# Another order of a chunk's cycle, and other moments for its loads, in an attention and expert kernel

## The chip, the cores and the metric

The kernel runs on one core of a Trainium2 chip. The metric is the device time of one execution in microseconds, launch to end, as the median of several runs. "Us" below are microseconds.

## What is computed

The reference is windowed causal attention with a linear bias over 8 batches of 8 heads, 576 positions and 64 dimensions, followed by a layer of 8 experts, of which each token goes to the one that its gate ranks first:

```python
scores = scale * np.matmul(q, k.transpose(0, 1, 3, 2))
bias = slopes[:, None, None] * (-np.abs(rel).astype(np.float32))[None, :, :]
mask = (rel >= 0) & (rel < 128)
attn = softmax(np.where(mask, scores + bias[None], -1e9))
x = np.matmul(attn, v)                     # as rows: (4608 tokens, 512)
expert_idx, gate_w = argmax and softmax value of x @ w_gate
out[mask_e] = gate_w * (np.maximum(x[mask_e] @ w1[e], 0) @ w2[e])   # for each expert e
```

## The kernel before

Attention goes by 36 chunks of 128 query rows, all 8 heads together. A pair of batches makes nine chunks: four blocks of the first batch, one "tail" chunk that holds the last 64 rows of both batches, four blocks of the second. A query row looks back 127 positions, so a chunk needs its own key block and the one before; the first block of a batch (chunks 0, 5, 9, 14, 18, 23, 27, 32) has no block before it, so its scores and its values are half as large.

The order of every engine's instructions is written out by hand. The program counts steps, four for a chunk, and each piece of a chunk's work has a step relative to the chunk's first (a "lag") and a rank within the step. What stands in one step on several engines is recorded in the order of the ranks, and each engine then runs its own list in that order, waiting on semaphores alone. The work of several chunks thus interleaves; with c the chunk that begins in a cycle of four steps, one cycle holds:

- **S0** and **S1**, the scores of heads 0 to 3 and 4 to 7 of chunk c (`scores`, L163: bias from a bf16 matmul against an identity, then query times key), each into a PSUM bank pair of its own, `s0_ps` and `s1_ps`, which each serve every chunk.
- **F0** and **F1** (`weigh`, L191): VectorE folds the two key blocks into one with a masked copy (L196; none in a first block) and takes the maximum (L199). **E0** and **E1**: ScalarE's four exponentials each (L205), the sum with them. E1 goes in two halves, one in chunks from 3 on ahead of the x copy, one behind.
- **T0** of chunk c-1 and **T1** of chunk c-2 (`transposes`, L217), into one of the two banks `b_ps` that take turns; **P0** and **P1** (`place`): ScalarE copies a transposed half to `pT` (L223), GpSimd masks it into its two key blocks (two selects, L231 and L233; none in a first block).
- **V**, the values of chunk c-2 (`av`, L249), 32 matmuls (16 in a first block) into a third `b_ps`, the first half of them from P0, the second from P1. **X**: ScalarE's copy of that bank to `xT` (L299).
- **R** of chunk c-4 (`rows`, L263), which brings x to rows and adds the gate's logits, and **Y** (L266), VectorE's multiply by the reciprocal of the sums (L256), with the logits' sum (L1252) and the store of x to HBM (L1258).

With two banks `b_ps` and the order T1, T0, V, each T0 takes the bank that the V of the cycle before wrote and X reads.

Beside that runs routing: every five or six chunks (`GROUPS`) a group's tokens are ranked in four pieces on VectorE (`route`, L484), one at the end of each of four cycles running, with a few matmuls on TensorE. GpSimd adds a small guard to the sums (L189) and scales queries (L77). From step 57 on the first expert's weights are split into two parts, half a tile a cycle: a cast on ScalarE (L1042), its remainder on GpSimd (L1047).

Loads and x stores stand on SyncE's queue in program order, so a load behind an x store is asked for when Y has run. Before, a batch's keys are asked for four chunks ahead in one load (`KA = 16` steps), query tiles four chunks ahead (`QA = 4`), value tiles at most one and three quarters of a cycle ahead of their use (`VA = 4` against a lag of 11).

From about 210 us on the experts run: first layer and second layer of each of them, 128 to 512 columns a matmul.

Of the kernel before, what the change touches and what calls it, by code (L numbers as in the profile page):

```python
# [22 lines left out]
NP = H // 2  # L23
# [17 lines left out]
def attention(ctx, tc, st, qT, kT, v, iw, load_c2, chunk_done, chunks, begun):  # L41
# [95 lines left out]

    k0 = load_k(0, (0, KCUT, 256, 384, S))
    next(k0)
# [12 lines left out]
    next(k0)  # L152
# [3 lines left out]
    list(k0)  # L156
# [34 lines left out]
    def weigh(g, pe, rsum, s_ps, m, tail, lo, hi, later=False, add=True):  # L191
# [20 lines left out]
        return exps if later else exps()  # L212
# [41 lines left out]
    def rows(ch, subs, xT, rsum):  # L254
        rinv = small.tile([128, H], F32, name="rinv")
        nc.vector.reciprocal(out=rinv, in_=rsum)  # L256
        st["r_ps"] = r_ps = ps_r.tile([128, 2, 512], F32, name="r_ps")
        heads = r_ps[:, :, 0:NP * HW].rearrange("q c (p x) -> q p c x", p=NP)
        half = lambda c: slice(64 * c, 64 * c + 64)
        for p in range(NP):  # L260
            for a in range(2):
                for c in range(2):
                    nc.tensor.matmul(out=heads[half(a), p, c, :], lhsT=xT[half(c), p, half(a)], rhs=iw_sb[half(c), p, :],  # L263
                                     start=True, stop=True)
        x_sb = xp.tile([128, NP, XW], F32, name="x_sb")
# [5 lines left out]
    ahead = {}  # L271
    done_q, done_v, scaled = {(0, 0), (0, 1), (0, 2)}, {(0, 0), (0, 1)}, {(0, 0)}
    for ch, subs in enumerate(chunks):
        for b, i in subs:
            k = (b, i // 4)
            for seen, f, at in ((done_q, load_q, 4 * (ch - QA)), (done_v, load_v, 4 * ch + VA - TA * (k[1] == 4)),
                                (scaled, lambda b, m: scale_q(nc.gpsimd, b, m), 4 * ch - 6)):
                for j in ((b, 3), k) if f == load_v and k[1] == 4 else (k,):
                    if j not in seen:
                        seen.add(j)  # L280
                        ahead.setdefault(max(0, at), []).append((f,) + j)
# [3 lines left out]
    lags = lambda ch: LAGS.get(ch, LAGS[None])  # L285
    plan = {}
    for ch in range(len(chunks)):
        for k, at in enumerate(lags(ch)):
            plan.setdefault(4 * ch + at, []).append((k, ch))
        for k, at in enumerate(SUMS.get(ch, ())):  # L290
            plan.setdefault(4 * ch + at, []).append((11 + k, ch))
        if ch in SPLIT:
            plan.setdefault(4 * ch + 3, []).append((10, ch))
        plan.setdefault(4 * ch + lags(ch)[1] + (ch in SPLIT), []).append((13, ch))
    live, pes, sums, pTs, xTs, xps, second, turned = {}, {}, {}, {}, {}, {}, {}, {}
# [5 lines left out]
    def do(k, ch):  # L301
        if k == 9:
            return copy_x(ch)
        if k == 13:
            return place(chunks[ch], 0, turned.pop(ch), pTs[ch])
        if k > 10:
            h = slice(4 * k - 44, 4 * k - 40)
            nc.vector.tensor_reduce(out=sums[ch][:, h], in_=pes[ch][:, h, :], axis=AX.X, op=ALU.add)
            return guard(sums[ch]) if k == 12 else None
        if k == 10:  # L310
            exps = second.pop(ch)
            exps((0,))
            copy_x(ch - 2)
            return exps((1,))
        subs = chunks[ch]
        if k in (0, 4):
            if k == 0:
                pes[ch] = pp.tile([128, H, 128], F32, name="pe")
                sums[ch] = small.tile([128, H], F32, name="rsum", bufs=8)
            live[ch] = scores(subs, k // 4)  # L320
        elif k in (2, 5):
            second[ch] = weigh(k // 3, pes[ch], sums[ch], *live.pop(ch), later=k == 5 and ch in SPLIT, add=ch not in SUMS)
        elif k == 1:
            pTs[ch] = ptp.tile([128, 2, H, 128], F32, name="pT")
            turned[ch] = transposes(0, pes[ch])
        elif k == 3:
            rows(ch, subs, xTs.pop(ch), sums.pop(ch))
        elif k == 6:
            place(subs, 1, transposes(1, pes[ch] if ch in SUMS else pes.pop(ch)), pTs[ch])
        elif k == 7:  # L330
            xps[ch] = bank() if ch else ps_r.tile([128, 2, 512], F32, name="r_ps")[:, 0].rearrange("q (p x) -> q p x", p=NP)
            av(subs, pTs[ch], xps[ch], range(NP // 2))
        else:
            av(subs, pTs.pop(ch), xps[ch], range(NP // 2, NP))
            if len(lags(ch)) < 10 and ch + 2 not in SPLIT:
                copy_x(ch)

    def rank(k, ch, s):
        if k == 9:
            return 0.5  # L340
        if k == 6 and s == 4 * ch + 8:
            return 1
        if k == 1 and ch in SPLIT:
            return 1.5
        if k == 13:
            return 3.5 if ch in SPLIT else 1
        return 4.5 if k == 6 and s == 4 * ch + 6 else k

    def step(s):
# [5 lines left out]
        for f, b, m in ahead.get(s, ()):  # L355
            f(b, m)
        for k, ch in sorted(plan.get(s, ()), key=lambda x: (rank(*x, s), x[1])):
            do(k, ch)
        if s < len(WU) - 1:
            warm_up(WU[s + 1])  # L360
        for k in list(st["stages"]):
            if k[1] <= s and (s in PACE[k[2]] if k[2] in PACE else s % 4 == 3):
                k[1] = s + 1
                if next(k[0], k) is k:
                    st["stages"].remove(k)
# [21 lines left out]
LAGS = {None: (0, 4, 0, 17, 2, 2, 8, 11, 11)}  # L387
LAGS.update({ch: (0, 4, 0, 17, 2, 2, 6, 11, 11) for ch in (1, 2)})
LAGS[0] = (0, 4, 0, 17, 2, 2, 6, 7, 11, 12)
LAGS.update({ch: (0, 4, 0, 17, 2, 2, 8, 9, 11) for ch in (4, 13, 22, 31)})  # L390
LAGS.update({33: (0, 4, 0, 15, 2, 2, 8, 11, 11), 34: (0, 4, 0, 13, 2, 2, 8, 10, 10), 35: (0, 4, 0, 10, 2, 2, 6, 8, 8)})
# [3 lines left out]
TA = 4  # L395
# [12 lines left out]
KCUT = 128  # L408
# [9 lines left out]
QA = 4  # L418
KA = 16
# [903 lines left out]
```

## Time and profile before

| what | value |
| --- | --- |
| median of the runs | 639.75 us (lowest 639.19) |
| the profiled execution, whole | 640.18 us |
| its span, first to last instruction | 638.5 us |
| TensorE busy | 616.4 us, 97% |
| VectorE busy | 390.1 us, 61% |
| ScalarE busy | 313.9 us, 49% |
| GpSimd busy | 301.7 us, 47% |

The shares are averages over attention and experts. In the attention part, from 105 to 135 us for instance, VectorE, ScalarE and GpSimd are busy 79, 87 and 75% of the time, while a busy TensorE means only that matmuls follow each other: their ends are modelled, so a hole is best read from the starts of the groups on both sides of it. TensorE's granted clock is full (1.00) throughout attention. "Issue" in a row means that the engine waited for nothing that the profile shows.

### The profile page before, as it was taken

Reading aid. Unit: us, or ns where it says so; the run is one execution under the profiler, and the core shown is the slowest. Engines: PE = TensorE matmul, PEld = TensorE weight load, DVE = VectorE, ACT = ScalarE, POOL = GpSimd, SP = SyncE. Lnnn points to the kernel's source line nnn. Section 1 sums busy time; section 2 is a strip of 40 time slices with the busy share of each in tenths; the row PEclk is TensorE's granted clock in tenths of the full one; section 3 lists DMA queues with packets and bytes.
Section 4 is the critical chain, followed back from the end, with each engine's and each line's share of the span. In section 5 each row is a group of like instructions: output and inputs, shape, how many; then the busy total and the mean of one; then the engine's idle time right before and its main releaser. Section 6 shows DMA issues by size and latency. Waiting matters only on the chain.

```text
span 638.5 us, 16747 instructions
## 1 busy us (share of the span) xinstructions
PE 616.4 (97%) x6544; PEld 527.1 (83%) x6544; DVE 390.1 (61%) x946; ACT 313.9 (49%) x939; POOL 301.7 (47%) x414
## 2 busy tenths in 40 slices
PE   8998999999898999999999999999999999999995
PEld 5776777777676988988989999899899998888884
DVE  7677888859888886545553664565465456356411
ACT  5877788888777324533342334334233333433311
POOL 5643557768554150076327616732760760580202
PEclk9999999999999999999999999999999999999999
DMA  8967898988644253473535325433543542544101
GB/s 310 303 164 213 212 266 234 216 260 229 169 99 118 68 166 87 163 257 103 190 104 181 105 78 181 122 92 128 160 106 101 173 126 78 182 120 138 65 1 61
DMA packets 58179, 97.85 MB, mean 153 GB/s; under 512 B 11685, under 2 KB 32421, under 8 KB 57202
## 3 DMA queue, kind: packets, MB, share of 16 engines
q1 hardware_dynamic: 49618, 76.74, 40.2%
q0 software_dynamic: 8336, 19.76, 11.0%
q8 instruction: 52, 0.85, 0.6%
q10 hardware_dynamic: 144, 0.26, 0.2%
q14 instruction: 29, 0.24, 0.1%
HBM read 77.76 MB, written 18.98 MB: 152 GB/s over the span
## 4 chain that ended last, share of the span: by engine, by line
PE 67%; DVE 2%; ACT 1%; issue 0%; POOLq 0%; POOL 0%; ACTq 0%
PE y_ps L936 32%; PE l_ps L735 30%; PE s_ps L735 1%; PE x_ps L692 1%; PE b_ps L249 1%; PE y_ps L895 1%; PE r_ps L263 1%; DVE x_sb L266 0%; ACT pe L205 0%; PE b_ps L217 0%; DVE nmax L199 0%; DVE s_ps L196 0%; PE x_ps L895 0%; ACT xT L299 0%; PE s_ps L692 0%
## 5 line engine op out<-in xcount | busy, mean ns | idle before, releaser
L738 ACT ACTIVATE hh<-l_ps 128x320 fp32r<-128x320 f32 (+4 forms) x104 | 46.5, 447 | 200.7 <-PE l_ps L735 200.7
L742 DVE SCALAR_TENSOR_TENSOR hl<-l_ps,hh 128x320 fp32r<-128x320 f32 (+4 forms) x104 | 52.2, 502 | 147.7 <-ACT hh L738 147.4
L715 POOL DMA_INDIRECT xg<-xd,od_idx x112 | 117.6, 1050 | 35.2 <-issue 33.8
L205 ACT ACTIVATE pe<-s_ps,nmax 128x128 f32<-128x128 f32 x288 | 102.4, 382 | 36.2 <-DVE nmax L199 30.9
L936 PE MATMUL y_ps<-wh,hh 128*128 128x512 f32 x280 | 110.0, 393 | 0.0
L936 PE MATMUL y_ps<-wl,hh 128*128 128x512 f32 x280 | 109.4, 391 | 0.0
L936 PE MATMUL y_ps<-wh,hl 128*128 128x512 f32 x280 | 109.2, 390 | 0.0
L924 POOL DMA_INDIRECT out<-y,od_pidx x33 | 34.4, 1043 | 147.8 <-ACT y L942 141.3
L1030 DVE TENSOR_TENSOR wl<-w_raw,wh 128x512 fp32r<-128x512 f32 x114 | 73.7, 688 | 30.0 <-ACT wh L1026 29.7
L735 PE MATMUL l_ps<-xh,wh 128*128 128x320 f32 (+8 forms) x416 | 81.0, 316 | 0.0
L735 PE MATMUL l_ps<-xl,wh 128*128 128x320 f32 (+8 forms) x416 | 80.4, 315 | 0.0
L735 PE MATMUL l_ps<-xh,wl 128*128 128x320 f32 (+8 forms) x416 | 80.3, 315 | 0.0
L735 PEld LDWEIGHTS l_ps<-xh,wh 128*128 128x128 f32 x416 | 67.8, 188 | 6.7 <-issue 1.2
L735 PEld LDWEIGHTS l_ps<-xl,wh 128*128 128x128 f32 x416 | 65.9, 188 | 1.9
L735 PEld LDWEIGHTS l_ps<-xh,wl 128*128 128x128 f32 x416 | 65.8, 188 | 2.0
L249 PE MATMUL b_ps<-pT,v_sb 128*64 128x128 f32 (+2 forms) x1136 | 65.6, 265 | 0.8 <-issue 0.6
L249 PEld LDWEIGHTS b_ps<-pT,v_sb 128*64 128x64 f32 (+1 forms) x1136 | 56.4, 137 | 10.4 <-issue 5.8
L936 PEld LDWEIGHTS y_ps<-wh,hl 128*128 128x128 f32 x280 | 52.6, 188 | 11.5
L1026 ACT CAST wh<-w_raw 128x1024 fp32r<-128x1024 f32 x57 | 59.5, 1043 | 3.8 <-DMA w_raw<-w 3.8
L936 PEld LDWEIGHTS y_ps<-wh,hh 128*128 128x128 f32 x280 | 52.6, 188 | 9.6 <-ACT hh L738 0.4
L936 PEld LDWEIGHTS y_ps<-wl,hh 128*128 128x128 f32 x280 | 52.6, 188 | 9.1
L183 PE MATMUL s_ps<-k_sb,q_sb 64*64 64x192 f32 (+2 forms) x1152 | 58.6, 307 | 1.3 <-issue 1.2
(227 smaller groups left out, 920.6 us busy)
## 6 DMA issues: line engine op xcount, KB each, us to landing
w_raw<-w SPq DMA_DIRECT2D x64, 512.0 KB, 3.9
q_sb<-qT SPq DMA_DIRECT2D x39, 256.0 KB, 5.7
xd<-x_sb SPq DMA_DIRECT2D x32, 258.0 KB, 5.2
v_sb<-v SPq DMA_DIRECT2D x32, 256.0 KB, 5.1
k_sb<-kT SPq DMA_DIRECT2D x7, 1152.0 KB, 8.9
w_n<-w SPq DMA_DIRECT2D x4, 1024.0 KB, 6.3
xg<-xd,od_idx POOLq DMA_INDIRECT x112, 3.0
xd<-x_sb SPq DMA_DIRECT2D x8, 129.0 KB, 4.3
```

The source lines that it names most:

```text
L183: nc.tensor.matmul(out=s_ps[halves(a), c, n, x0:x1], lhsT=blocks["q", b, m][h, 2 * g + n, qs], rhs=batch[b][h, 2 * g + n, k0:k0 + x1 - x0] ...
L205: nc.scalar.activation(out=pe[:, h, :], in_=s_ps[:, c, n, lo:lo + 128], func=AF.Exp, bias=nmax[:, 2 * c + n:2 * c + n + 1], scale=1.0, **( ...
L249: nc.tensor.matmul(out=x_ps[64 * c:64 * c + 64, p, q], lhsT=blocks["v", b, m - 1 + kb][0:kk, D * h:D * h + D], rhs=pT[0:kk, kb, h, q], sta ...
L263: nc.tensor.matmul(out=heads[half(a), p, c, :], lhsT=xT[half(c), p, half(a)], rhs=iw_sb[half(c), p, :], start=True, stop=True)
L715: ins = tc.nc.gpsimd.indirect_dma_start(out=g[:, s], out_offset=None, in_=parts, in_offset=bass.IndirectOffsetOnAxis(ap=idx[:, s], axis=0),)
L735: nc.tensor.matmul(out=ps, lhsT=a[:, 128 * d:128 * d + 128], rhs=b[:, d], start=(k == 0), stop=(k == 11))
L738: nc.scalar.activation(out=hh, in_=ps, func=AF.Relu)
L742: nc.vector.scalar_tensor_tensor(out=hl, in0=ps, scalar=0.0, in1=hh.bitcast(F32), op0=ALU.max, op1=ALU.subtract)
L924: ins = nc.gpsimd.indirect_dma_start(**kw).ins
L936: nc.tensor.matmul(out=ys[t], lhsT=a[:, tl], rhs=b[:, 512:1024], start=(f == 0 and k == 0), stop=(f == 7 and k == 2))
L1026: keep(tc, nc.scalar.copy(out=wh, in_=raw))
L1030: keep(tc, eng.tensor_tensor(out=wl[:, sl], in0=raw[:, sl], in1=wh.bitcast(F32)[:, sl], op=ALU.subtract))
```

## The change

The list of lags becomes a table of places, one (step, rank) for each piece. Nothing is computed otherwise. In a cycle from chunk 3 on:

- X goes right behind V, ahead of all of E1. The second half of E1 goes to the head of the next step, and P1 behind it, then P0, then E0.
- R, Y and S1 are recorded in the first step of the cycle; the order on TensorE stays S0, T1, T0, R, S1, V, but that the first half of a tail chunk's V, which stood ahead of S1 in four cycles, now stands behind it.
- Y goes ahead of the routing piece where that has a place of its own, and the reciprocal goes to the end of a cycle.
- The weight cast goes between E0 and X, its remainder on GpSimd behind both pairs of selects.
- A batch's keys come as four loads, each at a chunk's step of its own, 16 steps ahead of the first use of its columns; query tiles are asked for six chunks ahead at most, value tiles 18 steps ahead, or when their buffer comes free; weight tiles five steps earlier.

The core of the diff:

```diff
-    def load_k(b, cuts=(0, S)):
-        batch[b] = qkv.tile([128, NP, S], F32, name="k_sb", bufs=2)
-        for c, d in zip(cuts[:-1], cuts[1:]):
-            yield nc.sync.dma_start(out=batch[b][:, :, c:d], in_=kT[b][:, :, c:d])
+    def load_k(b, cut):
+        if b not in batch:
+            batch[b] = qkv.tile([128, NP, S], F32, name="k_sb", bufs=2)
+        nc.sync.dma_start(out=batch[b][:, :, cut[0]:cut[1]], in_=kT[b][:, :, cut[0]:cut[1]])
...
+    for key, load, have, bufs, lead, done in (("q", load_q, 3, QBUF, QA, 2), ("v", load_v, 2, VBUF, VA, 9)):
+        for n, (j, ch) in enumerate(needs[key]):
+            if n >= have:
+                free = 4 * uses[key][needs[key][n - bufs][0]] + done if n >= bufs else 0
+                at = max(free, 4 * (ch - lead) + done)
...
     for b in range(1, B):
-        at = 4 * next(ch for ch, subs in enumerate(chunks) if any(x == b for x, _ in subs))
-        ahead.setdefault(at - KA, []).append((lambda b, _: list(load_k(b)), b, 0))
+        at = 36 * (b // 2) + (0 if b % 2 else -16)
+        cuts = ((384, S), (0, 128), (128, 256), (256, 384)) if b % 2 else ((0, 128), (128, 256), (256, 384), (384, S))
+        for n, cut in enumerate(cuts):
+            behind.setdefault((4, 8, 10, 12)[n] if b == 1 else at + 4 * n, []).append((load_k, b, cut))
...
-        n, i = divmod(s - FETCH, 8)
-        if 0 <= n < 7 and i in (0, 3, 4, 7):
-            (st["rest_of"] if i % 4 else st["round"])(n, i // 4)
-        if (s - FETCH + 12) % 8 == 0 and 0 <= (s - FETCH + 12) // 8 < 8:
-            st["load"]((s - FETCH + 12) // 8)
+        for name, f in (("round", 0), ("rest_of", 3)):
+            at, rank = HOOKS[name]
+            n, i = divmod(s - FETCH - at, 4)
+            if i == 0 and 0 <= n < 14:
+                todo.append((rank, 0, lambda name=name, n=n: st[name](n // 2, n % 2)))
+        for _, _, f in sorted(todo, key=lambda x: x[:2]):
+            f()
+        if (s - FETCH + 17) % 8 == 0 and 0 <= (s - FETCH + 17) // 8 < 8:
+            st["load"]((s - FETCH + 17) // 8)
...
-LAGS = {None: (0, 4, 0, 17, 2, 2, 8, 11, 11)}
...
+PLACES = dict(S0=(0, 0), T1=(8, 1), T0=(4, 2), E11=(4, 3), R=(16, 4), P1=(8, 5), F0=(0, 6), S1=(0, 7), P0=(4, 8), Y=(16, 9),
+              E0=(1, 0), F1=(1, 1), V0=(11, 7), V1=(11, 7.2), I=(15, 8), X=(11, 9), E10=(3, 10))
+HOOKS = dict(Q=-1, L=18, G=20, round=(1, 11), rest_of=(2, 5.5))
...
-QA = 4
-KA = 16
+QA = 6
```

(E10 and E11 are the halves of E1, V0 and V1 those of V, I the reciprocal, Q the scaling of queries, L the loads, G the routing pieces.)

What the tables do to the lists shows on two engines. On ScalarE, one cycle in the middle of attention; `s0_ps` marks E0, `s1_ps` E1, `xT` is X, `pT` P1 and then P0, `wh` the weight cast. Before:

```order
L223 COPY pT_2362<-b_ps_2464 128x512
L205 ACTIVATE pe_2450,rsum_2451<-s0_ps_107,nmax_2479 128x128 x4
L223 COPY pT_2472<-b_ps_2473 128x512
L1042 CAST wh_2402<-w_raw_2032 128x512
L205 ACTIVATE pe_2450,rsum_2451<-s1_ps_108,nmax_2529 128x128 x2
L299 COPY xT_2550<-b_ps_2531 128x512
L205 ACTIVATE pe_2450,rsum_2451<-s1_ps_108,nmax_2529 128x128 x2
```

And after the change:

```order
L310 COPY xT_2332<-b_ps_2313 128x512
L205 ACTIVATE pe_2227,rsum_2228<-s1_ps_108,nmax_2302 128x128 x4
L223 COPY pT_2246<-b_ps_2373 128x512
L223 COPY pT_2378<-b_ps_2379 128x512
L205 ACTIVATE pe_2359,rsum_2360<-s0_ps_107,nmax_2406 128x128 x4
L1068 CAST wh_2445<-w_raw_1945 128x512
```

X has left the middle of E1 and leads it; P1 has moved from the head of the cycle to behind E1, and E0 to behind both copies.

On SyncE's queue, the loads of the cycles 4 to 6; `xd` is a store of x. Before:

```order
L1258 DMA xd_63<-x_sb_528 512x1x129
L73 DMA q_sb_576<-qT 128x512
L69 DMA k_sb_578<-kT 128x2304
L1258 DMA xd_63<-x_sb_633 512x1x129
L82 DMA v_sb_679<-v 128x512
L73 DMA q_sb_681<-qT 128x512
```

And after:

```order
L1284 DMA xd_63<-x_sb_651 512x1x129
L69 DMA k_sb_655<-kT 128x4x128
L82 DMA v_sb_663<-v 128x512
L73 DMA q_sb_666<-qT 128x512
L1284 DMA xd_63<-x_sb_755 512x1x129
L69 DMA k_sb_655<-kT 128x4x128
L73 DMA q_sb_785<-qT 128x512
```

A batch's keys stood behind one store as a whole (128 partitions of 2304 values); now a quarter stands behind each of four stores.

## Rows read from the trace of the kernel before

**Rows 1.** First line of the page: the span of the profiled execution.
```profile
span 638.5 us, 16747 instructions
```

**Rows 2.** TensorE's waits from 20 to 206 us: total us, times, longest us.
```profile
PE b_ps L217 <- ACT xT L299: 8.6, 17, 1.0
PE s_ps L183 <- issue: 1.2, 2, 1.0
PE r_ps L263 <- issue: 0.9, 1, 0.9
PE r_ps L557 <- DVE x_sb L266: 0.7, 1, 0.7
PE b_ps L249 <- issue: 0.6, 1, 0.6
```

**Rows 3.** TensorE in order of time, cycle 14: start us, us, instruction, [idle before].
```profile
76.36 0.30 PE L174 MATMUL s_ps<-bias_sb,eye_sb 64*64 64x256 bf16 x4
...
77.03 1.09 PE L217 MATMUL b_ps<-c_sb,pe 128*128 128x128 f32 x8
78.05 0.73 PE L263 MATMUL r_ps<-iw_sb,xT 64*64 64x72 f32 x32
78.60 0.29 PE L174 MATMUL s_ps<-bias_sb,eye_sb 64*64 64x256 bf16 x4
...
79.25 1.97 PE L249 MATMUL b_ps<-pT,v_sb 128*64 128x128 f32 x32
```

**Rows 4.** TensorE in order of time, a cycle behind short values.
```profile
113.50 1.09 PE L249 MATMUL b_ps<-pT,v_sb 128*64 128x128 f32 x16 [0.20 <-DMA v_sb<-v]
114.53 0.36 PE L174 MATMUL s_ps<-bias_sb,eye_sb 64*64 64x384 bf16 x4
...
115.46 0.66 PE L217 MATMUL b_ps<-c_sb,pe 128*128 128x128 f32 x4
117.14 0.66 PE L217 MATMUL b_ps<-c_sb,pe 128*128 128x128 f32 x4 [1.02 <-ACT xT L299]
117.72 0.48 PE L263 MATMUL r_ps<-iw_sb,xT 64*64 64x72 f32 x16
```

**Rows 5.** ScalarE in order of time, 107 to 117 us.
```profile
107.16 0.37 ACT L205 ACTIVATE pe<-s_ps,nmax 128x128 f32<-128x128 f32 x1 [0.60 <-DVE nmax L199]
...
108.55 0.59 ACT L223 COPY pT<-b_ps 128x512 f32<-128x512 f32 x1
...
115.80 0.37 ACT L205 ACTIVATE pe<-s_ps,nmax 128x128 f32<-128x128 f32 x1 [0.43 <-DVE p L535]
...
116.50 0.58 ACT L299 COPY xT<-b_ps 128x512 f32<-128x512 f32 x1
116.97 0.39 ACT L205 ACTIVATE pe<-s_ps,nmax 128x128 f32<-128x128 f32 x1
```

**Rows 6.** VectorE in order of time, 114 to 124 us.
```profile
114.30 0.69 DVE L196 COPY_PREDICATED s_ps<-mask_sb,s_ps 128x512 f32<-128x512 uint32 x1
...
115.63 0.15 DVE L535 SCALAR_TENSOR_TENSOR p<-t,rank 128x5 f32<-128x5 f32 x1
...
117.22 0.68 DVE L196 COPY_PREDICATED s_ps<-mask_sb,s_ps 128x512 f32<-128x512 uint32 x1
...
119.81 0.69 DVE L196 COPY_PREDICATED s_ps<-mask_sb,s_ps 128x512 f32<-128x512 uint32 x1
...
123.47 0.42 DVE L196 COPY_PREDICATED s_ps<-mask_sb,s_ps 128x256 f32<-128x256 uint32 x1
```

**Rows 7.** GpSimd's groups by line, 60 to 165 us: busy us, mean ns.
```profile
L231 POOL TENSOR_SCALAR_AFFINE_SELECT pT<-pT 128x512 f32<-128x512 f32 x28 | 17.9, 638 | 13.8 <-ACT pT L223 13.8
L1047 POOL TENSOR_TENSOR wl<-w_raw,wh 128x512 fp32r<-128x512 f32 x14 | 17.9, 1276 | 0.0
```

**Rows 8.** DMA issues by line: count, KB each, median us to landing.
```profile
k_sb<-kT SPq DMA_DIRECT2D x7, 1152.0 KB, 8.9
...
k_sb<-kT SPq DMA_DIRECT2D x3, 256.0 KB, 5.4
```

More of the change, by code (lines that the diff above doesn't have):

```diff
@@ L269, in rows @@
         chunk_done(ch, subs, x_sb)
-    ahead = {}
-    done_q, done_v, scaled = {(0, 0), (0, 1), (0, 2)}, {(0, 0), (0, 1)}, {(0, 0)}
+    ahead, behind = {}, {}
+    needs = {"q": [], "v": []}
+    uses = {"q": {}, "v": {}}
     for ch, subs in enumerate(chunks):
[L274 to L281, printed above, removed]
+        for b, i in subs[::2]:
+            m = i // 4
+            for key, tiles in (("q", ((b, m),)), ("v", ((b, m - 1), (b, m)) if m else ((b, m),))):
+                for j in tiles:
+                    if j not in uses[key]:
+                        needs[key].append((j, ch))
+                    uses[key][j] = ch
@@ new lines, in attention @@
+    for key, load, have, bufs, lead, done in (("q", load_q, 3, QBUF, QA, 2), ("v", load_v, 2, VBUF, VA, 9)):
[3 more added lines that the diff above has]
+                at = max(free, 4 * (ch - lead) + done)
+                assert at < 4 * ch + done - 4, (key, j, ch, at)
+                behind.setdefault(at, []).append((load,) + j)
+    for j, ch in needs["q"][1:]:
+        ahead.setdefault(max(0, 4 * ch - 6), []).append((lambda b, m: scale_q(nc.gpsimd, b, m),) + j)
@@ L301, in do @@
     def do(k, ch):
[L302 to L314, printed above, removed]
@@ L315, in do @@
         subs = chunks[ch]
-        if k in (0, 4):
-            if k == 0:
+        g = int(k[1]) if k[1:].isdigit() else 0
+        if k in ("S0", "S1"):
+            if g == 0:
                 pes[ch] = pp.tile([128, H, 128], F32, name="pe")
                 sums[ch] = small.tile([128, H], F32, name="rsum", bufs=8)
[L320 to L347, printed above, removed]
+            live[ch, g] = scores(subs, g)
+        elif k in ("F0", "F1"):
+            weighed[ch, g] = weigh(g, pes[ch], sums[ch], *live.pop((ch, g)), add=ch not in SUMS)
+        elif k in ("E0", "E1"):
+            weighed.pop((ch, g))()
+        elif k == "E10":
+            weighed[ch, 1]((0,))
+        elif k == "E11":
+            weighed.pop((ch, 1))((1,))
+        elif k in ("A0", "A1"):
+            nc.vector.tensor_reduce(out=sums[ch][:, 4 * g:4 * g + 4], in_=pes[ch][:, 4 * g:4 * g + 4, :], axis=AX.X, op=ALU.add)
+            if g:
+                guard(sums[ch])
+        elif k in ("T0", "T1"):
+            if ch not in pTs:
+                pTs[ch] = ptp.tile([128, 2, H, 128], F32, name="pT")
+            turned[ch, g] = transposes(g, pes[ch])
+        elif k in ("P0", "P1"):
+            place(subs, g, turned.pop((ch, g)), pTs[ch])
+        elif k in ("V0", "V1"):
+            if g == 0:
+                xps[ch] = bank() if ch else ps_r.tile([128, 2, 512], F32, name="r_ps")[:, 0].rearrange("q (p x) -> q p x", p=NP)
+            av(subs, pTs[ch], xps[ch], range(2 * g, 2 * g + 2))
+        elif k == "X":
+            copy_x(ch)
+        elif k == "I":
+            rinvs[ch] = inverse(sums.pop(ch))
+        elif k == "R":
+            heads[ch] = rows(xTs.pop(ch))
+        elif k == "Y":
+            scale_rows(ch, subs, heads.pop(ch), rinvs.pop(ch))
@@ L349, in step, with pieces @@
+    def pieces(due):
+        for k in list(st["stages"]):
+            if k[1] <= st["step"] and due(k[2]):
+                k[1] = st["step"] + 1
+                if next(k[0], k) is k:
+                    st["stages"].remove(k)
     def step(s):
```

74 lines of the change are left out of this document (40 added, 34 removed).

## The prediction, made before the changed kernel ran

> **What bounds the kernel now.** The profiled execution spans 638.5 us [rows 1]; its own time is 640.18, so 1.7 us lie around the span, and the median of the runs is 639.75, 0.4 below it. TensorE counts as busy for nearly all of it (the table above), so a gain can only come out of its holes, and between the start and the last store these lie in the attention part, from 20 to 206 us. I read TensorE's waits of that stretch first: the largest by far is the second group of transposes, T0, waiting for ScalarE's x copy, 17 times and 8.6 us [rows 2]. Then I read TensorE in order of time around one such hole, to see what a hole really costs: T0 and T1 together take 1.02 us where nothing stops them (77.03 to 78.05) [rows 3], and 2.26 us (115.46 to 117.72) around a hole of 1.02 [rows 4]. A hole thus costs its idle time and another 0.22, and the 17 cost 8.6 + 17 x 0.22 = 12.3 us.
>
> Why T0 waits: there are two transpose banks and three users a cycle (T1, T0, values), so T0 of this cycle takes the bank that the values of the cycle before filled and X has to empty. ScalarE does X only between the two halves of the second softmax, and these wait for VectorE's fold and maximum of the second scores. From the end of S1 the chain is: about 0.2 until VectorE starts (an estimate, the size of the 0.22 above), fold and maximum 1.50 (114.30 to 115.80) [rows 5, 6], two exponentials 0.70, X until T0 starts 0.64 (116.50 to 117.14) [rows 4, 5]: 3.04 us. TensorE's work meanwhile is the values 1.91 (1.97 busy, less the 0.06 by which the 1.09 of a short one exceeds its 1.03), S0 0.93 and T1 0.51: 3.35. That leaves 0.3. Behind a first block (16 instead of 32 value matmuls, 1.03) the chain is 0.57 too long, and likewise in the four tail cycles, where half the values stand ahead of S1. These are 11 of the 17 holes. The others come where VectorE is late, because a routing piece stands ahead of the fold, like the 1.59 from 115.63 to 117.22, or the 2.33 up to 123.47 that follow the fold and maximum of 119.81 (1.33, as from 114.30 to 115.63) [rows 6].
>
> **The change, part by part.** *TensorE's order* moves only in the four tail cycles; its work stays. A regular cycle is S0 0.93, T 1.02, rows 0.55, S1 0.93, values 1.91 = 5.34 us; 4.46 with short values; 4.80 where the scores are a first block's (0.67 and 0.65) [rows 3, 4].
>
> *X right behind the values.* X now starts about 0.2 after the values end, and T0 can go 0.2 + 0.64 = 0.84 after them; TensorE gets there after S0 and T1, 1.44. All 17 holes at T0 should close: 12.3 us.
>
> *What is late next.* All four second exponentials now stand behind X, and the copy P1 and both selects of P1 on GpSimd behind them. Counting from the end of the values: X at 0.2, exponentials from 0.67 (X to the next start is 0.47), 1.39 for four, done at 2.1 [rows 5]. S1 of the next chunk needs that bank at 0.93 + 1.02 + 0.55 = 2.50: 0.4 to spare, and 0.15 in a first-block cycle (2.24). P1 takes 0.59, the two selects 1.28 (638 ns each) [rows 5, 7]: ready at 4.05 with 0.1 for the semaphores, while the second half of the values is reached at 2.50 + 0.93 + 0.95 = 4.38: 0.3 to spare. In a first-block cycle it is reached at 3.84, so 0.21 is lost, in 7 of them 1.5 us. ScalarE's own list is X 0.47, eight exponentials 2.8 and two copies 1.2, 4.5 of 5.34 us before the weight cast, so it holds little reserve beyond these. The cast moves to the place ahead of X, where ScalarE would wait for the values anyway, and costs nothing there. The first three chunks and the last three nearly keep their places; I count nothing for them.
>
> *VectorE.* The second fold must now be done by the time X is: in a regular cycle that is 1.91 + 0.67 - 0.2 - 1.50 = 0.9 after the earliest moment, with the 0.3 above 1.2 us, where it was 0.3. Behind short values it is 0.3. A VectorE cycle is 1.33 for a fold with its maximum and 2.59 for the rest (117.22 to 119.81) [rows 6], 3.92; with a piece 5.5 to 6.25. Four pieces come in four cycles running, so VectorE falls behind by 0.2 to 0.9 in a regular cycle and by up to 1.8 in a 4.46 one, and each group of chunks meets one of those. The reserve takes most: I leave 0.6 us for each of five groups, and 0.9 more for the group whose shift of counts stands there too: 4.0 us. The row multiply Y now stands ahead of the last routing piece of that group; TensorE's wait there for Y, 0.7 with its 0.2, goes [rows 2].
>
> *Loads.* Before, keys came as 1152 KB at once; after, as four pieces one cycle apart, values and queries asked for about 4.5 and 5.5 cycles ahead. TensorE has four holes released by "issue", 1.2 + 0.9 + 0.6 = 2.7 us idle [rows 2], with 4 x 0.22 some 3.6. Two of them open while a whole key load is under way, the other two one cycle later; no semaphore of the profile ends them, so I take it that instructions are missing. If their fetches queue behind the key packets, smaller pieces shorten the holes. Bounds are 0 and 3.6; I take 2.2, as the pieces leave the queues a quarter as full but not empty. The Trainium skill's "Runtime: NRT & Kernel Launch" (Instruction fetch mechanics) says an engine fetches its instructions in 16 KiB blocks over its own DMA queue and that the cost is mostly hidden. By that rule the loads would have nothing to give; the four holes speak against it, at least here, without showing the fetch itself.
>
> Against the pieces speaks how they land: a whole key load 8.9 us after its issue, a 256 KB piece after 5.4 [rows 8], so four cost at least 21.6 in turn. Each has four cycles, 21 us, before its use, so this lies beside other work; without that cover it would be a stall of 5 us for each of seven batches. "DMA: Bandwidth & Descriptors" in the Trainium skill (Rules for kernel authors) asks for at least 1 MiB in one DMA; the landing times agree, and by them alone the split would lose.
>
> **Sum.** 12.3 + 0.9 + 2.2 - 1.5 - 4.0 = 9.9 us. From 640.2 that is 630.3, and 0.4 lower for the median: 629.9. What follows attention stays TensorE's and hides nothing, so a gain arrives whole.
>
> **Rivals.** *Nothing late in exchange:* VectorE's pieces and the selects are absorbed and all issue holes close: 12.3 + 0.9 + 3.6 = 16.8, 623. For it speaks the reserve of 1.2 us at the fold, four times the old one; against it VectorE's 5.5 to 6.25 us in every cycle with a piece.
>
> *Mere exchange:* the waits move from T0 to S1 and to the second half of the values, with both costing twice the 5.5 that I took and no hole by issue closing: 13.2 - 11.0 = 2.2, 637.5. For it: ScalarE's list in a fixed order, and VectorE's cycles with a piece as above. Against: behind the values, where 11 of the 17 holes come from, X no longer waits for VectorE at all.
>
> *Slower:* GpSimd gets to P1's selects too late. Its cycle holds four selects, 2.6, and half a weight remainder, 1.3 [rows 7], besides guard and query scaling, and a loop closes over it: values end, X, four exponentials, P1, selects, second half of values, 0.2 + 0.47 + 1.39 + 0.59 + 1.38 + 0.95 = 5.0 against 5.34. From 0.35 us of delay in each cycle on, the loop decides; at 0.9 a cycle, some 30 cycles cost 0.55 each, 16.5 against 15.4 gained: 641. Against it: the weight remainder moves from ahead of a select to behind both.
>
> *The loads do nothing:* the four holes stay, the sum without 2.2, 632; this lies inside the first case, and I give it one in three there. The Trainium skill's "Runtime: NRT & Kernel Launch" (Instruction fetch mechanics), as cited above, would have it so.
>
> **How the numbers follow.** Forecast 0.5 (626 to 634), nothing late 0.2 (620 to 626), exchange 0.2 (634 to 640), slower 0.1 (above 640). The time is the forecast's, 629.9. The range 622 to 637 leaves out a quarter of the second case, half of the third and the fourth. Two per cent, about what a measurement of this kernel can tell from no change, is 12.8 us: under 627 lie the second case and a tenth of the first, 0.26; above 652.5 only the slower one grown threefold, 0.02.
>
> **What would show it.** Right: no T0 wait for X among TensorE's waits; S1 waiting for ScalarE's exponentials or the values for GpSimd's selects, some 5 us in all and mostly in cycles with routing pieces; fewer holes by "issue"; the last-layer part as long as before. Wrong: waits at S1 in regular cycles without a piece (the loop over ScalarE), waits for k_sb, q_sb or v_sb (the pieces too slow), issue holes as large as before, or VectorE's pieces longer than 2.3 us.

## The result, and the profile after

The changed kernel takes 632.92 us in the median (631.79 to 634.14), where the kernel before took 639.75 (639.19 to 642.80) on the same chip: a ratio of 0.988, 95% interval 0.984 to 0.993. One more run of the kernel before took 2106.82 us and counts nowhere here. A second measurement gave 0.989 (0.988 to 0.991). In time that is 7 to 8 us, where 9.9 were forecast; 632.9 lies inside the range of 622 to 637 and 3.0 above the forecast of 629.9. The profiled execution took 632.43 us. All views of this section are of the changed kernel, and the first is the head of its page, which answers to [rows 1]:

```profile
span 630.7 us, 16748 instructions
```

TensorE's waits from 20 to 206 us (total us, times, longest us), answering to [rows 2]:

```profile
PE s_ps L174 <- DVE s_ps L196: 2.5, 4, 1.2
PE s_ps L174 <- ACT pe L205: 1.5, 4, 0.5
PE b_ps L249 <- issue: 0.6, 2, 0.4
PE r_ps L583 <- DVE x_sb L272: 0.5, 1, 0.5
PE r_ps L583 <- DVE rr L577: 0.2, 1, 0.2
```

T0's 17 waits for the x copy are gone, and of the 2.7 us of holes by "issue" 0.6 is left. New are eight waits of a first score group, S0 (line 174 begins both score groups; by the order of time all eight are S0's). The wait for VectorE's row multiply, 0.7 before, is still there as 0.5 and 0.2. TensorE in order of time around the longest new wait (start us, us, instruction, [idle before]), answering to [rows 3, 4]:

```profile
87.43 0.34 PE L174 MATMUL s_ps<-bias_sb,eye_sb 64*64 64x384 bf16 x4
...
88.35 1.09 PE L249 MATMUL b_ps<-pT,v_sb 128*64 128x128 f32 x16
90.68 0.36 PE L174 MATMUL s_ps<-bias_sb,eye_sb 64*64 64x384 bf16 x4 [1.23 <-DVE s_ps L196]
...
91.62 1.09 PE L217 MATMUL b_ps<-c_sb,pe 128*128 128x128 f32 x8
92.64 0.73 PE L261 MATMUL r_ps<-iw_sb,xT 64*64 64x72 f32 x32
```

T1 and T0 take 1.02 us (91.62 to 92.64) behind short values too, where they took 2.26 in [rows 4]. Instead S0 stands still for 1.23. ScalarE at that place, answering to [rows 5]: the first and the last exponential of E0, then the weight cast and X.

```profile
89.12 0.37 ACT L205 ACTIVATE pe<-s_ps,nmax 128x128 f32<-128x128 f32 x1 [0.80 <-DVE nmax L199]
...
90.17 0.37 ACT L205 ACTIVATE pe<-s_ps,nmax 128x128 f32<-128x128 f32 x1
90.51 0.63 ACT L1068 CAST wh<-w_raw 128x512 fp32r<-128x512 f32 x1
91.02 0.61 ACT L310 COPY xT<-b_ps 128x512 f32<-128x512 f32 x1
```

E0 waits 0.80 for VectorE's first maximum, and its last exponential ends at 90.54, 0.14 before S0 starts in the same bank. In all eight waits S0 starts 0.14 after the end of E0's last exponential, also in the four that the profile puts down to a fold on VectorE; it is E0 that S0 waits for. VectorE (answering to [rows 6]) and GpSimd (to [rows 7]) in the same stretch:

```profile
85.85 0.90 DVE L561 SCALAR_TENSOR_TENSOR p<-t,rank 128x5 f32<-128x5 f32 x1
86.78 0.83 DVE L563 TENSOR_TENSOR lp<-c_sb,p 128x640 bf16<-128x640 f32 x1
...
87.68 0.68 DVE L196 COPY_PREDICATED s_ps<-mask_sb,s_ps 128x512 f32<-128x512 uint32 x1
88.40 0.69 DVE L199 TENSOR_REDUCE nmax<-s_ps 128x4 f32<-128x512 f32 x1
...
91.41 1.10 DVE L570 TENSOR_TENSOR c<-c,t 128x5 f32<-128x5 f32 x1
...
93.19 0.73 DVE L577 TENSOR_TENSOR rr<-eq,c_sb 128x240 bf16<-128x240 f32 x2
```

```profile
85.46 1.27 POOL L1073 TENSOR_TENSOR wl<-w_raw,wh 128x512 fp32r<-128x512 f32 x1 [2.20 <-ACT wh L1068]
...
91.22 1.27 POOL L1073 TENSOR_TENSOR wl<-w_raw,wh 128x512 fp32r<-128x512 f32 x1 [0.89 <-ACT wh L1068]
```

Here is the cause that the prediction did not have. A routing piece begins at 85.85 with an instruction on five numbers per partition. The same instruction took 0.15 in [rows 6] (115.63); here it takes 0.90 and ends at 86.75. GpSimd's weight remainder runs from 85.46 to 86.73. The next piece begins at 91.41 with 1.10 and ends at 92.51; the remainder ends at 92.49. So VectorE's instruction ends only when GpSimd's is over, 0.75 to 1.0 us late (such an instruction takes 0.11 to 0.15 where nothing holds it), and the first fold F0, E0 and S0 stand behind it. That the one causes the other is tested below (e4, e12).

The key pieces' landings, answering to [rows 8], are 1 us slower than the 5.4 there, and TensorE never waits for one from 20 us on:

```profile
k_sb<-kT SPq DMA_DIRECT2D x24, 256.0 KB, 6.4
```

### The profile page after: what moved, and what is told of

It is laid out like the page before. It is cut to its first block, busy times and chain, and to the rows that moved or that the text cites. A ratio compares the mean times of both kernels' runs of the same rounds, so it can differ in the third digit from the quotient of the medians.

```text
span 630.7 us, 16748 instructions
## 1 busy us (share of the span) xinstructions
PE 614.7 (97%) x6544; PEld 529.4 (84%) x6544; DVE 393.1 (62%) x946; ACT 313.1 (50%) x939; POOL 300.8 (48%) x414
## 4 chain that ended last, share of the span: by engine, by line
PE 82%; DVE 9%; ACT 4%; issue 2%; DMA 1%; POOLq 0%; POOL 0%; SPq 0%; DVEq 0%; ACTq 0%
PE y_ps L962 32%; PE l_ps L761 31%; PE b_ps L249 6%; PE s_ps L183 3%; ACT pe L205 3%; PE b_ps L217 3%; DVE s_ps L196 2%; PE r_ps L261 2%; DVE nmax L199 2%; DVE x_sb L272 2%; PE s_ps L761 1%; PE s_ps L174 1%; DMA k_sb<-kT 1%; PE x_ps L718 1%; PE y_ps L921 1%
## 5 line engine op out<-in xcount | busy, mean ns | idle before, releaser
L205 ACT ACTIVATION_READ_ACCUMULATOR pe<-s_ps,nmax 128x1 f32 x264 | 59.5, 225 | 0.0
```

The source lines that it names most:

```text
L205: nc.scalar.activation(out=pe[:, h, :], in_=s_ps[:, c, n, lo:lo + 128], func=AF.Exp, bias=nmax[:, 2 * c + n:2 * c + n + 1], scale=1.0, **( ...
```

## The experiments

Each ratio is to runs of the kernel before on the same chip; 0.001 is 0.64 us. The other columns are worked out from the traces, one trace a kernel. "Last layer" is when its first second-layer product starts (the first y_ps of TensorE's order of time): where attention's gain can be read without the layer behind it. "S0 + S1" is idle time at line 174 from 20 us on: what stands behind row products is S1's, the rest S0's; one number alone is S0's. Transposes and values are the times of these groups from start to next start, 7 us to the last row product; of the values the idle time that the profile shows is taken off. "Held" is what VectorE's routing pieces lose to the remainder: instructions from 40 to 200 us that take 0.15 or more beyond the shortest of their line and end within 0.1 us of a remainder's end; in brackets how many. Such a meeting is called a collision below.

| run | ratio (95%) | last layer | S0 + S1 | transposes | values | held |
|---|---|---|---|---|---|---|
| before, first trace | | 225.47 | 0 | 50.6 | 63.4 | 1.2 (2) |
| e8 before again | 0.9994 (0.9984 to 1.0004) | 223.68 | 0 | 49.8 | 63.6 | 1.2 (2) |
| changed, first trace | 0.9881 (0.9836 to 0.9926) | 216.95 | 4.0 | 38.2 | 66.3 | 7.7 (9) |
| e5 changed again | 0.9893 (0.9878 to 0.9908) | 216.65 | 3.7 + 0.7 | 38.3 | 65.4 | 7.6 (9) |
| e1 X between | 0.9967 (0.9950 to 0.9985) | 221.58 | 0.9 | 50.0 | 64.2 | 6.9 (9) |
| e2 keys whole | 0.9894 (0.9873 to 0.9915) | 217.84 | 2.3 + 0.6 | 38.2 | 65.5 | 6.8 (9) |
| e3 before, keys in pieces | 0.9974 (0.9962 to 0.9987) | 222.18 | 0 | 51.6 | 63.4 | 1.2 (2) |
| e4 remainder behind | 0.9881 (0.9849 to 0.9912) | 214.70 | 1.5 + 0.5 | 38.2 | 65.7 | 4.4 (6) |
| e6 P1 first | 1.0019 (1.0010 to 1.0028) | 225.33 | 1.2 + 10.0 | 38.2 | 64.3 | 6.8 (8) |
| e7 P1 first, remainder behind | 0.9993 (0.9984 to 1.0002) | 223.23 | 0 + 9.6 | 38.2 | 63.8 | 3.7 (6) |
| e9 T1 first | 0.9922 (0.9908 to 0.9936) | 217.55 | 0.6 + 0.8 | 43.3 | 64.7 | 7.3 (9) |
| e10 T1 first, remainder behind | 0.9884 (0.9868 to 0.9901) | 214.74 | 0 + 0.7 | 42.3 | 64.9 | 3.7 (5) |
| e11 T1 first, remainder between | 0.9862 (0.9842 to 0.9883) | 213.77 | 0 + 0.8 | 42.6 | 64.4 | 1.4 (2) |
| e12 remainder between | 0.9842 (0.9825 to 0.9858) | 212.24 | 0.2 + 0.6 | 38.2 | 65.0 | 1.6 (2) |

The S1 waits of 0.5 to 0.8 in e2, e4, e5 and e9 to e12 are one wait each, near the end of attention (188 to 194 us). In e5 and e12 VectorE itself stands idle for 0.7 and 0.6 ahead of the fold that this wait hangs on, so it is not a late routing piece; no experiment here says what it is.

**Is the gain X's place? (e1)** One number: X's rank in its step, so that it comes between the two halves of E1.

```
-              E0=(1, 0), F1=(1, 1), ..., X=(11, 9), E10=(3, 10))
+              E0=(1, 0), F1=(1, 1), ..., X=(11, 10.5), E10=(3, 10))
```

> The changed kernel with the x copy X put back between the two halves of the second exponentials on ScalarE; everything else, the loads too, as changed. Theory (the gain is the T0 term: T0 waits for the bank that X empties, and X waits for VectorE's second fold): T0's waits for X come back, 8 to 10 us idle in 15 or more places, and TensorE's transpose groups between the start and the end of attention grow by 10 to 13 us again; the new waits of S0 (4.0 us) shrink in exchange by 1 to 3. Time 640 to 643, 8 to 10 above the changed kernel's 632.4. Rival (the gain is that of the loads or of VectorE's order, and X would have cost nothing where it stood): T0's waits under 3 us, time 632 to 635.

TensorE's waits from 20 to 206 us in e1:

```profile
PE b_ps L217 <- ACT xT L310: 8.1, 15, 1.7
PE s_ps L174 <- ACT pe L205: 0.6, 1, 0.6
...
PE s_ps L174 <- DVE s_ps L196: 0.3, 1, 0.3
```

T0's waits are back, with 11.7 us of transposes, as the theory had it. But the time rose by 4.7 only (0.9967 against 0.9893; 4.9 at the last layer), not by 8 to 10, and the median of 638.69 lies under the 640 to 643 expected: the waits of S0 and S1 fell by 3.5, the values by 1.2, and 0.7 of waiting at a routing product went. X's place is most of the gain, and it is a gross gain of 12 of which more than half is paid back.

**What are the key pieces worth? (e3, e2)** e3 is the kernel before with its keys split, and nothing else; e2 the changed kernel with the keys whole from batch 2 on.

```
e3 (before)
-        ahead.setdefault(at - KA, []).append((lambda b, _: list(load_k(b)), b, 0))
+        for n, cut in enumerate(...the changed kernel's four cuts...):
+            ahead.setdefault((4, 8, 10, 12)[n] if b == 1 else at - KA + 4 * n, []).append((..., b, cut))
e2 (changed)
-        for n, cut in enumerate(cuts):
+        for n, cut in enumerate(cuts if b == 1 else ((0, S),)):
```

> The kernel before with one thing of the change alone: the keys in four pieces, one cycle apart, asked for at the moments of the changed kernel; cycle order, query, value and weight loads as before. Theory (TensorE's instructions come late behind a whole key load): the holes released by nothing that the profile shows go from 2.7 us idle to 0.5 to 1.0, and the time falls by 2 to 4, ratio 0.994 to 0.997. Rival (the holes come from something else): 2 to 3 us of such holes and a ratio of 0.999 to 1.001. In both cases T0's waits for X stay at 8 to 9.5 us.

> The changed kernel with the keys of batches 2 to 7 loaded as one transfer of 1152 KB each again, asked for when the first of the four pieces is now; queries, values and weights asked for as changed. Theory (TensorE's instructions come late behind a whole key load): its holes released by nothing that the profile shows come back, from 0.6 us idle to 2 to 3, and the time is 634 to 636.5, 2 to 4 above 632.4. Rival (the holes went because the other transfers moved or because of the new order): 0.6 to 1.2 us of such holes, 631.5 to 633.5.

TensorE's waits from 20 to 206 us, of e3 first (all that there are), then the ones by "issue" of e2:

```profile
PE b_ps L218 <- ACT xT L302: 9.0, 17, 1.0
PE r_ps L560 <- DVE x_sb L267: 0.7, 1, 0.7
PE r_ps L570 <- DVE x_sb L267: 0.3, 1, 0.3
```

```profile
PE s_ps L183 <- issue: 0.9, 2, 0.7
PE b_ps L249 <- issue: 0.7, 1, 0.7
...
PE r_ps L261 <- issue: 0.4, 1, 0.4
```

Splitting the keys alone closes every hole by "issue" and is worth 1.7 us (0.8 to 2.4), just under what was expected; whole keys bring 2.0 us of them back. There the time does not move as expected (0.9894 against 0.9893 in the changed kernel; the last layer 1.2 later), while S0's waits shrink by 1.4: a hole while VectorE is late need cost nothing more, though that was not tested by itself. So the size of the key loads opens and closes most of these holes, and the pieces are worth 1.7 us in the kernel before; in the changed one the times show no gain.

**What does S0 wait for? (e4)** The remainder goes behind both pairs of selects of the next cycle.

```
-HOOKS = dict(Q=-1, L=18, G=20, round=(1, 11), rest_of=(2, 5.5))
+HOOKS = dict(Q=-1, L=18, G=20, round=(1, 11), rest_of=(3, 8.5))
```

> The changed kernel with GpSimd's weight remainder (1.27 us) moved from behind the weight cast to behind both pairs of selects of the next cycle; nothing else. In the changed kernel's trace seven routing pieces on VectorE begin with an instruction of 0.5 to 1.16 us where the same one takes 0.11 to 0.2 elsewhere, and each of these ends within 0.06 us of the end of a remainder on GpSimd. Theory (the two engines block each other, so the piece is late, then the first fold, its exponentials and S0): these instructions fall to 0.1 to 0.6 us, S0's waits from 4.0 us to under 1.5, and the time to 628.5 to 630.5, 2 to 4 below 632.4. First rival (VectorE is too full in a cycle with a piece in any case): the instructions shrink, but S0 still waits 3 us or more; 631.5 to 633. Second rival (the remainder now holds up GpSimd's selects): the value products wait for the selects 2 us more in all, 633 to 636.

S0's waits fall from 3.7 to 4.0 down to 1.5, close to what the theory has, and the last layer starts 2.0 to 2.2 earlier; but the time of 628.5 to 630.5 is missed (632.33), and the ratio of 0.9881 can't be told from the changed kernel's. Six collisions instead of nine are left, because behind the selects the remainder often still meets the piece. (The 13.3 us of stretched instructions named in later expectations count every instruction over 0.25 beyond the shortest, whoever ended it; the changed kernel has 15.5 by that count.) The trace shows the direction, the times don't show a gain.

**Do the values wait for P1's selects? (e6, e7)** P1 goes between the halves of E1 on ScalarE; in e7 the remainder moves as in e4 too.

```
-PLACES = dict(..., E11=(4, 3), R=(16, 4), P1=(8, 5), F0=(0, 6), ...)
+PLACES = dict(..., E11=(4, 3), R=(16, 4), P1=(8, 2.5), F0=(0, 6), ...)
```

> The changed kernel with the copy P1 on ScalarE moved from behind all four second exponentials to between their halves; nothing else. Theory (the value products wait for the selects of P1, 2.6 us in all): the selects begin 0.5 to 0.7 earlier, value products take 1.90 instead of 2.03 to 2.65, and TensorE's value groups shrink by 1.5 to 2.5 us in all; in exchange S1 waits for the exponentials, 0.1 to 0.3 in first-block cycles, 0.5 to 2 us in all. Time 631.5 to 633 where the changed kernel has 632.5. Rival (the value products wait for something else, or GpSimd is held up by VectorE anyway): value groups as long as before, S1 waits in addition, 633 to 634.5.

> Both moves together: the copy P1 between the halves of the second exponentials, and GpSimd's weight remainder behind both pairs of selects of the next cycle. Theory (VectorE's routing pieces are held up by the remainder): the selects come 0.5 to 0.7 earlier than with the remainder's move alone, so the remainder is over when the piece begins; the time that VectorE's piece instructions take beyond their shortest falls from 13.3 us (remainder moved) to under 8, S0's waits from 2.2 to under 1.2 us, and the time to 629.5 to 631.5, 1 to 3 below the changed kernel on the same chip. Rival (S1's waits for the exponentials eat it): within 1 us of the changed kernel.

Both lose the whole gain of the change, which neither case of either expectation had: 643.0 and 641.5 us, and e6 is slower than the kernel before. TensorE and ScalarE in order of time in e6, one cycle:

```profile
59.73 1.09 PE L217 MATMUL b_ps<-c_sb,pe 128*128 128x128 f32 x8
60.75 0.73 PE L261 MATMUL r_ps<-iw_sb,xT 64*64 64x72 f32 x32
61.77 0.36 PE L174 MATMUL s_ps<-bias_sb,eye_sb 64*64 64x384 bf16 x4 [0.28 <-ACT pe L205]
```

```profile
60.42 0.58 ACT L223 COPY pT<-b_ps 128x512 f32<-128x512 f32 x1 [0.22 <-PE b_ps L217]
60.91 0.37 ACT L205 ACTIVATE pe<-s_ps,nmax 128x128 f32<-128x128 f32 x1
...
61.26 0.37 ACT L205 ACTIVATE pe<-s_ps,nmax 128x128 f32<-128x128 f32 x1
...
61.60 0.59 ACT L223 COPY pT<-b_ps 128x512 f32<-128x512 f32 x1
```

P1 first waits 0.22 for T1 and then puts its own copy ahead of two exponentials, so S1's bank comes free at about 61.7, while TensorE is done with the rows at 61.3 (60.75 and 0.55): 1.02 from rows to S1 instead of 0.55. S1 waits so in 30 cycles, and the rows' total is some 36 us instead of 21 to 22. That is the loop over ScalarE of the prediction's "wrong" list; its reserve of 0.4 is real, and the 0.7 by which P1 delays the second half of E1 here (0.22 of waiting, then 0.49 until 60.91) uses it up in nearly every cycle and leaves the 0.28 of idle time. In e7 the collisions fall to 3.7 us and S0 waits nowhere, and S1's waits eat all of it. The values fall to 64.3 and 63.8, as expected if they wait for the selects; but the cycle is longer here and gives them room anyway, so that part is supported and not shown.

**Room for S0 (e9, e10)** T1 goes ahead of S0 on TensorE; in e10 the remainder moves as in e4 too.

```
-PLACES = dict(S0=(0, 0), T1=(8, 1), T0=(4, 2), ...)
+PLACES = dict(S0=(0, 0), T1=(8, -0.5), T0=(4, 2), ...)
```

> The changed kernel with TensorE's first group of transposes, T1, ahead of S0 in each cycle instead of behind it; the other engines' orders are the same. Theory (S0 waits because VectorE's first fold and with it the exponentials E0 are late behind a routing piece): S0 comes 0.51 us later behind the values and T0 at the same moment as now, so seven of the eight waits of 0.19 to 0.47 go and that of 1.23 falls to about 0.7; S0's waits from 4.0 to 4.7 us to about 1.0, no T0 waits, the first product of the second layer 2 to 3.5 us earlier, time 629.5 to 631.5 where the changed kernel has 632.5 (ratio 0.983 to 0.986). Rival (VectorE is the bound in these cycles, whatever stands on TensorE): S0's folds start 0.5 later too and the same time is lost at S1 or the values; ratio 0.987 to 0.990.

> The changed kernel with T1 ahead of S0 and GpSimd's weight remainder behind both pairs of selects. Theory (both act on the same waits, one on VectorE's delay and one on the room for it): S0's waits under 0.6 us, first product of the second layer at 213.0 to 214.5 us, time 628.5 to 631, ratio 0.981 to 0.985. Rival: as the better of the two moves alone, ratio 0.985 to 0.988.

TensorE in order of time in e9:

```profile
61.96 0.66 PE L217 MATMUL b_ps<-c_sb,pe 128*128 128x128 f32 x4
62.55 0.36 PE L174 MATMUL s_ps<-bias_sb,eye_sb 64*64 64x384 bf16 x4
...
63.48 0.66 PE L217 MATMUL b_ps<-c_sb,pe 128*128 128x128 f32 x4
64.07 0.73 PE L261 MATMUL r_ps<-iw_sb,xT 64*64 64x72 f32 x32
```

S0's waits went as expected, from 3.7 to 0.6 in e9 and to none in e10. Still e9 is slower than the changed kernel (0.9922, 0.9908 to 0.9936, against 0.9893), and e10 can't be told from it (0.9884); both lie outside what was expected. Four transposes by themselves take 0.59 (61.96 to 62.55) and 0.59 (63.48 to 64.07), eight in a row 1.02: 0.16 a cycle, and 43.3 us in all instead of 38.3. I had counted the move as free. It is also an answer to what S0 waits for: with 0.5 us of room in every cycle seven of its eight waits are gone in e9 and all in e10, as a late E0 would have it.

**Remainder between the selects (e11, e12)** The remainder stands behind P1's selects and ahead of P0's, which the next cycle's values need and not this one's; so it runs beside VectorE's folds. e11 with T1 first, e12 without.

```
-HOOKS = dict(Q=-1, L=18, G=20, round=(1, 11), rest_of=(2, 5.5))
+HOOKS = dict(Q=-1, L=18, G=20, round=(1, 11), rest_of=(3, 5.2))
```

> As the one before, but with the remainder between GpSimd's selects of P1 and those of P0. Theory (VectorE is held up only by instructions that stand beside its piece, and its folds, which read the score banks, run beside the remainder): the remainder lies beside the folds altogether, no instruction of a piece ends with a remainder, and what holds pieces up are selects of 0.64 us; VectorE's stretched instructions 13.3 us (remainder behind both pairs) to 7 to 11; ratio 0.981 to 0.985, within 0.002 of the one before. Rival (the folds too are held up by the remainder): folds of 1.2 us and more instead of 0.69, S0's waits over 3 us, ratio 0.987 or more.

> The changed kernel with the remainder between GpSimd's selects of P1 and those of P0, and T1 where the change put it, behind S0; so one move against the changed kernel. Theory (the collision of remainder and routing piece is what S0 waits for, and T1 ahead of S0 cost 4 to 5 us of TensorE's time in transposes): transposes take 38.2 us in all again instead of 42.6, S0's waits are 0.5 to 2.0 instead of 4.0 to 4.7, the first product of the second layer comes at 212.5 to 214.5 us (216.65 and 216.95 in the changed kernel), ratio 0.983 to 0.987. Rival (the value products must wait for the later selects of P0, or S0's waits have another source): first product at 215.5 or later, ratio 0.987 to 0.990.

e11 takes 0.9862, a little slower than expected, with two collisions left and no wait of S0, but with transposes of 42.6 us; e12 has them back at 38.2. VectorE and GpSimd of e12 at the piece that was shown above for the changed kernel:

```profile
83.34 0.11 DVE L561 SCALAR_TENSOR_TENSOR p<-t,rank 128x5 f32<-128x5 f32 x1
...
87.00 0.69 DVE L196 COPY_PREDICATED s_ps<-mask_sb,s_ps 128x512 f32<-128x512 uint32 x1
...
88.44 0.47 DVE L570 TENSOR_TENSOR c<-c,t 128x5 f32<-128x5 f32 x1
```

```profile
85.74 1.27 POOL L1073 TENSOR_TENSOR wl<-w_raw,wh 128x512 fp32r<-128x512 f32 x1
86.97 0.63 POOL L231 TENSOR_SCALAR_AFFINE_SELECT pT<-pT 128x512 f32<-128x512 f32 x1
...
88.28 0.62 POOL L77 TENSOR_SCALAR q_sb<-q_sb 128x512 f32<-128x512 f32 x1
```

The first instruction of the piece takes 0.11 instead of 0.90. That of the next piece takes 0.47 instead of 1.10 and ends at 88.91, with the query scaling (88.90) and not with a remainder. A fold at 87.00 runs its usual 0.69 beside a select. TensorE's waits of e12 from 20 to 206 us, and the longer of the two at line 174 in order of time:

```profile
PE s_ps L174 <- ACT pe L205: 0.8, 2, 0.6
PE s_ps L183 <- issue: 0.4, 2, 0.2
```

```profile
187.11 0.73 PE L261 MATMUL r_ps<-iw_sb,xT 64*64 64x72 f32 x32
188.43 0.36 PE L174 MATMUL s_ps<-bias_sb,eye_sb 64*64 64x384 bf16 x4 [0.59 <-ACT pe L205]
```

That wait stands behind row products, so it is S1's. With this one number S0's 3.7 to 4.0 us fall to 0.2, and e12 takes 631.09 us at a ratio of 0.984 (0.983 to 0.986): faster than the changed kernel (0.989, 0.988 to 0.991) by 0.5%, some 3.3 us. It is the best kernel of the study. The collision of remainder and piece is what S0 waited for: where the remainder stands decides it, and over the changed kernel, e4 and e12 S0's waits fall with the time held (7.7, 4.4 and 1.6 us).

**The two kernels again (e8, e5)**

> The kernel before unaltered, to read its trace on the chip of the experiments. Theory (its holes released by nothing that the profile shows come from the key loads, and the last layer's length differs between chips or runs): four holes or so again, 2 to 3.5 us idle from 20 to 206 us, within a key load or one cycle behind it; T0 waits for X 8 to 9.5 us; the stretch from the first product of the second layer to the end of the span is 414.5 to 416.5, not 413.0. Rival (chance): holes elsewhere, or under 1.5 us of them.

> The changed kernel unaltered, beside the others of this call, so that differences of 1 to 3 us can be read on the same chip. Theory (the last layer's length differs between chips or runs and not between these kernels): the stretch from the first product of the second layer (y_ps) to the end of the span, 413.7 us in the changed kernel's first trace and 414.8 to 416.4 in the four experiments so far, is 414.5 to 416.5 here too, and the ratio is 0.987 to 0.991. Rival (the last layer is longer in the experiments because of what they change): 413.5 to 414.0.

TensorE's first product of the second layer and the holes from 20 to 206 us of e8; then the same product of e5:

```profile
223.68 0.48 PE L936 MATMUL y_ps<-wh,e_hh 128*128 128x512 f32 x1
...
PE r_ps L263 <- issue: 1.0, 1, 1.0
...
PE s_ps L183 <- issue: 0.7, 1, 0.7
...
PE b_ps L249 <- issue: 0.3, 1, 0.3
```

```profile
216.65 0.48 PE L962 MATMUL y_ps<-wh,e_hh 128*128 128x512 f32 x1
```

From there to the end of the span it is 415.9 and 415.8 us (spans 639.6 and 632.5), and 413.0 and 413.7 in the first two traces: that length goes with the chip or the run, and the whole gain is made in attention. The kernel before has three holes here, 2.0 us, but not all where they were expected: that of 0.7 lies at 93 us, 17 us behind the issue of a key load and ahead of the next, with loads of 256 KB of values and queries and one of weights issued in the 11 us ahead of it. So a key load under way is not needed for such a hole. T0 waits for X 7.6 us there, a little less than expected.

## Why the prediction was right, and where it was not

Term by term, against the first pair of traces and against e8 and e5 (us; minus is a gain):

| term of the sum | forecast | first traces | e8, e5 |
|---|---|---|---|
| T0's holes (transposes) | -12.3 | -12.4 | -11.5 |
| holes by "issue", idle | -2.2 | -2.1 | -1.8 |
| TensorE's wait for Y | -0.9 | 0.0 | 0.0 |
| values waiting for selects | +1.5 | +2.9 | +1.8 |
| late folds (waits of S0 and S1) | +4.0 | +4.0 | +4.4 |
| sum | -9.9 | -7.6 | -7.1 |
| span | | -7.8 | -7.1 |
| start of the last layer | | -8.5 | -7.0 |

In the first pair the sum falls 0.9 short of what attention gained, 8.5; no term covers that.

- **X right behind the values.** Right in place and size: no T0 wait is left, and e1 brings them back. The 0.22 added to each hole was needed: the idle time alone is 8.6.
- **S1 keeps 0.4 in reserve.** Right: S1 waits nowhere in the first trace of the changed kernel and once (0.7, near the end) in e5, and e6 shows what happens without the reserve.
- **Values and selects.** Value groups took 1.8 to 2.9 longer, not 1.5. The sum had the seven first-block cycles alone, at 0.21 each; these lost 0.65 in all. The rest lies in tail cycles, where 64 products take 2.36 to 2.65 instead of 2.2 to 2.4, and in some regular ones (1.97 to 2.09 instead of 1.90); 0.64 of the 2.9 stands around the two holes by "issue". So the term came near by luck. With P1 early (e6) six of the seven first-block groups take 1.02 or 1.03 again, as in the kernel before; but no releaser is named inside these groups, so that all of it is the selects stays unproved.
- **VectorE's late folds.** The size, 4.0, was right by luck; place and reason were not. The prediction expected S1 to wait for the second fold, because a piece and two folds fill VectorE's cycle. It was S0 that waited for the first fold, and the pieces were late because GpSimd's remainder was now beside them: nine collisions of 7.7 us instead of two of 1.2. The step that failed is the price of the cast's move: "costs nothing there" counted ScalarE only, and the remainder that follows the cast on GpSimd was counted for the selects alone. With nearly all collisions gone (e12) 0.2 of S0's waits and 0.6 of S1's are left, so the reason given would by itself have cost at most a fifth of what was set down for it.
- **Y ahead of the piece.** Wrong by 0.9: the same routing product still waits, for Y 0.5 and for rr 0.2.
- **Loads.** The holes shrank by 2.1 and 1.8 where 2.2 was set down, and late fetches were the right mechanism: the trace shows the packets, which the prediction had not looked for (last section). In time the pieces alone bring 1.7 (e3).
- **The rivals.** "Nothing late in exchange" fell to the collisions. The truth lies between the forecast and "mere exchange", nearer to the forecast: 6.9 of 12.4 and 6.2 of 11.5 were paid back, 55%, where the forecast had 5.5 of 13.2 (42%) and that rival 11.0 (83%), and the larger part of it at S0, where neither had it. The loop over GpSimd did not close: most regular value groups take the 1.90 of the kernel before. "The loads do nothing" is excluded by e3.
- **What would have shown it wrong.** Pieces longer than 2.3 us were on that list and came: 91.41 to 93.92 is 2.5 (the lines on VectorE above). The list pointed at the right place; the sum had no term for it.

## What to carry to other kernels

When an instruction is moved on one engine, follow what it releases on the next engine and look at what a third one does at that moment: here a cast moved on ScalarE put a GpSimd instruction beside VectorE's, and one number that moved it on (e12) gave back 3.3 us. Put GpSimd's work beside VectorE's instructions that read the score banks, not beside those that work on small tiles in SBUF. And price a reordering on TensorE by what a group costs alone, not by its share of a longer run.

## What the runs showed of the hardware

- **A VectorE instruction can be held until one on GpSimd is over.** In the changed kernel instructions on 5 to 48 numbers per partition took up to 1.16 us instead of 0.11 to 0.2 and ended 0.01 to 0.06 after a GpSimd instruction, nine times a remainder (1.27), else mostly a select or the query scaling (0.6). Maximum and fold, which read the score banks, never took more than 0.70 in attention in any of the 14 traces, whatever GpSimd did. The Trainium skill's "SBUF — State Buffer" (Who interferes with whom) says that a VectorE instruction with two SBUF inputs contends with a GpSimd instruction that reads SBUF, that the shared port is an exclusive lock, and that a reduction doesn't contend: the trace agrees. Some held instructions have only one tensor as input, like the TENSOR_SCALAR of L606 on 128x6 (1.16 us, in e4 as short as 0.17), so two inputs are not the only case.
- **TensorE's holes by "issue" stand where its instructions come late.** The page of the kernel before has a DMA queue for instructions (packets, MB, share of 16 engines):

```profile
q8 instruction: 52, 0.85, 0.6%
```

  In the trace each of its packets has 16,384 bytes. Up to 140 us the 14 traces have 14 such holes of 0.15 us or more. They begin at ten places of TensorE's list of matmuls, from number 981 to 2759, which lie on a grid of 126 to 128; number 981 has a hole in the kernel before, in e8 and in e1. Counted along the list, each place has its packet, and at the holes this packet is late: it is complete 3.9 to 6.0 us after the place before it was reached, elsewhere after 3.1 in the median. In 13 of the 14 holes the next matmul starts 1.3 to 1.7 us after that, in one 2.1. A matmul here is a weight load and a product, so the grid is about 256 instructions. The Trainium skill's "Runtime: NRT & Kernel Launch" (Instruction fetch mechanics) gives 16 KiB or 256 instructions as the block that an engine fetches at a time, and calls the cost mostly hidden. Block and grid agree; hidden it is at most places, but four of the kernel before cost 0.26 to 0.98 us, and one of e8 1.04.
- **Short groups of transposes are dear.** Four take 0.59 us between other work, eight in a row 1.02 (e9).
